# Inverse roots of batch 0's last two chunks on VectorE in Newton steps, with a new order of the whole kernel

## The chip, the core and the metric

One core of one Trainium2 chip runs the kernel. It has five engines that work side by side: TensorE (PE: matrix products, with weight loads, PEld, that overlap them), VectorE (DVE), ScalarE (ACT), GpSimd (POOL) and SyncE (SP, which here only issues transfers), and 16 DMA engines that move data. Every engine works through its own list of instructions in order; semaphores hold an instruction back until what it needs is there. The metric is the device time of one launch, in microseconds (us).

## The reference

For each of 8 batches and 8 heads, with 576 tokens of 64 numbers, a linear attention is computed and normalised by its root mean square; the heads are put side by side to 512 channels, and a gated linear unit with a causal convolution of 5 taps follows.

```python
kv  = einsum('bhsd,bhse->bhde', k, v)
out = einsum('bhsd,bhde->bhse', q, kv)
rms = sqrt(mean(out * out, axis=-1, keepdims=True) + 1e-06)
x   = out / rms * g_norm                     # then (B, S, H*D) = (8, 576, 512)

gate_pre = sum_k conv_w[k] * xp[:, k:k + S, :]   # xp: x with 4 zero rows ahead
gate = 1 / (1 + exp(-gate_pre))
val  = x @ w_val
return gate * val @ w_out
```

All numbers are float32, but the three weights come as float64, which the kernel narrows itself, in integer operations (`narrow_weight`).

## The kernel before

**Order.** The whole kernel is one list of named steps, `PLAN`, written out by a planner and run once, from first to last, under a manual schedule. A step issues its instructions on one engine (a DMA on a queue), and the place of a step in the list is its place on its engine. So the list fixes the order on every engine; nothing else moves.

**Chunks.** A batch's 576 tokens are cut into four whole chunks of 128 tokens, 0 to 3, and a last one, 4, of 64 tokens, whose eight heads are folded so that it fills 128 partitions with four heads each. In a step such as `sums 0 3` the first number is the batch and the second the chunk.

**One batch, step by step.**
- `load_half` (k and v), `load_q` or `load_q_rows`: loads, on SP's queue except a few on ScalarE's at the start. Only three blocks of q fit, and a load of q waits until the block that it overwrites has been turned.
- `kv_product b i` (PE, L435) makes k'v into the bank pair `raws`, and `kv_copy` (ACT, L443) copies it to SBUF.
- q is turned so that its head dimension lies on the partitions: for batches 0 and 1 by PE (`turn_q_rows`, L469, then `sort_q` on ACT, L476), for the others by VectorE (`turn_q`, L455).
- `raw_product` (L490) or `raw_pair` (L507), PE: q times kv, a chunk or a pair of them.
- `square` (ACT, L525) squares a chunk into one of two buffers, whose 65th column holds the epsilon; `sums` (DVE, L533) adds over each head, 8 numbers per token (4 for chunk 4); `powers` (POOL, L539) raises them to the power -0.5; `normalise` multiplies raw by the result: for batch 0 on VectorE (L555), for the others on ScalarE, a head at a time (L551).
- x is turned to channels on partitions: by PE (`turn_x`, L566, one PSUM buffer) and ScalarE (`keep_x`, L573) for batches 0 and 1 and for every chunk 4; otherwise by VectorE (`turn_blocks`, L579) and four DMAs on GpSimd's queue (`move_blocks`, L587).
- `halo` (POOL, L594) fills the rows ahead of the first token.
- The gate: `gate_start` (ACT, L598), four `gate_tap` (DVE, L604), `gate_end` (ACT, sigmoid, L611).
- The values: `val_product` and `keep_val` for batches 0 and 1 (PE L616, ACT L625); from batch 2 on seven products in place of eight by sums of operands (`val_fast`, L666; `x_sums`, `val_sums`, `val_keep`). `gated` (DVE, L629) multiplies by the gate.
- The output product: `out_product` (L697, L704), in the second half `fast_product` with sums (L763), then `keep_out` or `fast_keep`, and `store`.

**Around the change.** In batch 0 PE has little else to do while the first chunk goes from raw to x: the order on PE is the five raw products, `turn_x 0 3`, `turn_x 0 2`, `kv_product 1 0`, `turn_x 0 4`, two `turn_q_rows 1`, `turn_x 0 1`, and so on to the first `val_product 0 0 1`, whose weights `narrow_weight wval 0 0` to `0 7` must be done. `keep_warm` (L426) issues products that nobody uses; one stands ahead of `kv_product 0 1`, one behind it. The GpSimd list there is `powers 0 3`, `0 2`, `0 4`, `0 1`, `0 0`, `halo 0`. A number of `powers` results waits in one of three buffers.

Of the kernel before, what the change touches and what calls it, by code (L numbers as in the profile page):

```python
# [9 lines left out]
FP32 = mybir.dt.float32  # L10
# [5 lines left out]
P = 128  # L16
# [5 lines left out]
turn_q_rows 0 1; sort_q 0 0; narrow_weight cw 0 0; turn_q_rows 0 2; narrow_weight cw 0 1; narrow_weight cw 0 2;  # L22
turn_q_rows 0 3; narrow_weight cw 0 3; sort_q 0 1; narrow_weight cw 0 4; narrow_weight cw 0 5; turn_q_rows 0 4;
sort_q 0 2; narrow_weight cw 0 6; kv_product 0 0; narrow_weight cw 0 7; load_q_rows 1 0; sort_q 0 3;
load_half k 1 0; sort_q 0 4; load_half v 1 0; load_q_rows 1 1; keep_warm 1; kv_product 0 1; load_half k 1 1;
stage_weight wval 2; keep_warm 1; turn_cw; stage_weight wval 3; kv_copy 0; narrow_weight wval 1 0; load_half v 1 1; keep_cw;
narrow_weight wval 1 1; raw_product 0 3; load_half v 2 0; raw_product 0 2; square 0 3;
narrow_weight wval 1 2; raw_product 0 4; sums 0 3; load_half k 2 0; square 0 2; raw_product 0 1;
narrow_weight wval 0 0; powers 0 3; narrow_weight wval 1 3; sums 0 2; narrow_weight wval 0 1; raw_product 0 0;
load_half k 2 1; square 0 4; square 0 1; sums 0 4; powers 0 2; normalise 0 3; stage_weight wout 0; square 0 0;  # L30
narrow_weight wval 0 2; narrow_weight wval 1 4; turn_x 0 3; sums 0 1; narrow_weight wval 0 3; powers 0 4;
keep_x 0 3; normalise 0 2; narrow_weight wval 1 5; turn_x 0 2; powers 0 1; normalise 0 4; kv_product 1 0;
narrow_weight wval 1 6; keep_x 0 2; sums 0 0; turn_x 0 4; narrow_weight wval 0 4; turn_q_rows 1 0; powers 0 0;
keep_x 0 4; normalise 0 1; turn_q_rows 1 1; narrow_weight wval 0 5; sort_q 1 0; narrow_weight wval 1 7;
turn_x 0 1; halo 0; sort_q 1 1; normalise 0 0; turn_q_rows 1 2; keep_x 0 1; narrow_weight wval 2 0;
narrow_weight wval 0 6; narrow_weight wval 2 1; turn_x 0 0; narrow_weight wval 0 7; sort_q 1 2;
turn_q_rows 1 3; narrow_weight wval 3 0; narrow_weight wval 2 2; keep_x 0 0; turn_q_rows 1 4;
narrow_weight wval 2 3; kv_product 1 1; load_q 2 0; sort_q 1 3; narrow_weight wval 2 4; gate_start 0 0;
val_product 0 0 1; kv_copy 1; gate_tap 0 0 3; load_half v 2 1; sort_q 1 4; narrow_weight wval 3 1;
gate_tap 0 0 2; load_q 2 1; gate_start 0 1; raw_product 1 3; narrow_weight wval 2 5; gate_tap 0 0 1;  # L40
keep_val 0 0 1; raw_product 1 2; square 1 3; gate_tap 0 0 0; gate_start 0 2; val_product 0 1 1; sums 1 3;
square 1 2; narrow_weight wval 2 6; gate_end 0 0; powers 1 3; load_q 2 2; gate_tap 0 2 3;
narrow_weight wval 3 2; raw_product 1 1; sums 1 2; narrow_weight wval 3 3; gate_tap 0 1 3; raw_product 1 0;
keep_val 0 1 1; powers 1 2; stage_weight wout 2; square 1 1; normalise 1 3; val_product 0 0 0; sums 1 1;
narrow_weight wval 2 7; powers 1 1; gate_tap 0 2 2; square 1 0; turn_x 1 3; normalise 1 2; gate_tap 0 2 1;
val_product 0 1 0; sums 1 0; narrow_weight wout 0 0; keep_x 1 3; powers 1 0; narrow_weight wval 3 4;
narrow_weight wout 0 1; turn_x 1 2; narrow_weight wval 3 5; keep_val 0 0 0; raw_product 1 4; turn_q 2 0;
keep_x 1 2; kv_product 2 0; keep_val 0 1 0; narrow_weight wval 3 6; load_q 2 3; normalise 1 1; gate_tap 0 2 0;
kv_product 2 1; narrow_weight wval 3 7; square 1 4; stage_weight wout 3; val_sums 0; normalise 1 0; sums 1 4;
turn_x 1 1; turn_q 2 1; powers 1 4; val_product 0 2 1; keep_x 1 1; turn_q 2 2; load_q 3 0;  # L50
narrow_weight wout 0 2; gated 0 0; narrow_weight wout 0 3; turn_x 1 0; gate_tap 0 1 2; val_product 0 2 0;
keep_x 1 0; narrow_weight wout 2 0; gate_tap 0 1 1; load_half k 3 0; normalise 1 4; narrow_weight wout 0 4;
narrow_weight wout 2 1; turn_x 1 4; narrow_weight wout 0 5; val_product 0 3 1; gate_end 0 2; turn_q 2 3;
kv_copy 2; gate_tap 0 1 0; keep_x 1 4; keep_val 0 2 1; narrow_weight wout 0 6; raw_pair 2 3; keep_val 0 3 1;
narrow_weight wout 0 7; gate_start 0 3; stage_weight wout 1; load_half k 3 1; val_product 1 0 1; square 2 3;
load_q 3 1; narrow_weight wout 2 2; sums 2 3; square 2 2; narrow_weight wout 3 0; powers 2 3; gate_end 0 1;
gate_tap 0 3 3; val_product 0 3 0; narrow_weight wout 2 3; sums 2 2; keep_val 0 2 0; gated 0 1; load_q 3 2;
powers 2 2; narrow_weight wout 2 4; val_product 1 0 0; normalise 2 3; gate_tap 0 3 2; narrow_weight wout 2 5;
load_half v 3 0; gated 0 2; keep_val 0 3 0; halo 1; val_product 1 1 1; normalise 2 2; narrow_weight wout 2 6;
gate_tap 0 3 1; load_half v 3 1; narrow_weight wout 2 7; narrow_weight wout 3 1; raw_pair 2 1; turn_q 3 0;  # L60
keep_val 1 0 0; keep_val 1 0 1; narrow_weight wout 3 2; raw_product 2 4; narrow_weight wout 1 0;
turn_blocks 2 3; square 2 1; val_product 1 1 0; narrow_weight wout 1 1; load_q 3 3; sums 2 1; square 2 0;
turn_blocks 2 2; powers 2 1; narrow_weight wout 1 2; turn_q 3 1; val_product 1 2 1; square 2 4;
narrow_weight wout 3 3; sums 2 0; narrow_weight wout 1 3; narrow_weight wout 3 4; powers 2 0; gate_start 1 0;
gate_tap 0 3 0; val_product 1 2 0; normalise 2 1; narrow_weight wout 1 4; narrow_weight wout 1 5; sums 2 4;
normalise 2 0; val_product 1 3 1; narrow_weight wout 1 6; powers 2 4; narrow_weight wout 3 5; turn_blocks 2 1;
gate_end 0 3; narrow_weight wout 3 6; kv_product 3 0; keep_val 1 1 1; narrow_weight wout 1 7; normalise 2 4;
gate_tap 1 0 3; kv_product 3 1; gate_start 1 2; load_half k 4 0; gated 0 3; load_q 4 0; keep_val 1 1 0;
turn_blocks 2 0; turn_x 2 4; kv_copy 3; val_product 1 3 0; turn_q 3 2; gate_start 1 1; narrow_weight wout 3 7;
keep_val 1 2 1; gate_tap 1 0 2; keep_x 2 4; out_product 0 1; move_blocks 2 3; keep_val 1 3 0; gate_tap 1 1 3;  # L70
keep_val 1 2 0; turn_q 3 3; gate_tap 1 0 1; load_q 4 2; gate_tap 1 1 2; gate_tap 1 0 0; raw_pair 3 3;
load_half v 4 0; gate_tap 1 2 3; gate_end 1 0; out_product 0 0; gate_tap 1 1 1; square 3 2; keep_out 0 1;
gated 1 0; move_blocks 2 2; square 3 3; store 0 1; sums 3 2; gate_start 1 3; gate_tap 1 2 2; keep_val 1 3 1;
sums 3 3; out_product 0 2; gate_tap 1 1 0; keep_out 0 0; load_q 4 1; powers 3 3; gate_tap 1 3 3; gate_end 1 1;
gate_tap 1 2 1; load_half k 4 1; powers 3 2; gate_tap 1 2 0; normalise 3 3; gate_tap 1 3 2; out_product 0 3;
gated 1 1; store 0 0; gate_end 1 2; move_blocks 2 1; gate_tap 1 3 1; normalise 3 2; gate_tap 1 3 0; gated 1 2;
gate_end 1 3; raw_pair 3 1; gated 1 3; turn_q 4 0; raw_product 3 4; square 3 0; out_product 0 4; val_sums 1;
keep_out 0 3; load_q 4 3; square 3 1; sums 3 0; sums 3 1; square 3 4; powers 3 0; keep_out 0 2;
turn_blocks 3 3; store 0 3; weight_sums 0; weight_sums 1; out_product 0 7; powers 3 1; normalise 3 0;
val_sums 2; load_half v 4 1; weight_sums 2; turn_q 4 1; move_blocks 2 0; turn_blocks 3 2; turn_q 4 2;  # L80
store 0 2; normalise 3 1; out_product 0 5; sums 3 4; powers 3 4; keep_out 0 4; load_q 5 0; turn_blocks 3 1;
halo 2; turn_blocks 3 0; val_sums 3; kv_product 4 0; keep_out 0 5; turn_q 4 3; normalise 3 4; x_sums 2 0;
kv_product 4 1; load_half v 5 0; gate_start 2 2; x_sums 2 1; store 0 4; turn_x 3 4; gate_tap 2 2 3; kv_copy 4;
val_fast 2 0 0; keep_x 3 4; gate_tap 2 2 2; gate_start 2 1; val_fast 2 0 1; move_blocks 3 3; x_sums 2 2;
val_keep 2 0 0; load_q 5 1; keep_out 0 7; raw_pair 4 3; x_sums 2 3; gate_start 2 0; val_fast 2 0 2; square 4 3;
gate_tap 2 0 3; val_keep 2 0 1; store 0 5; sums 4 3; val_fast 2 0 3; val_keep 2 0 2; gate_tap 2 0 2;
square 4 2; powers 4 3; val_fast 2 0 4; sums 4 2; load_half k 5 0; val_fast 2 0 5; val_keep 2 0 4;
# [751 lines left out]
```

## Time and profile before

| | |
|---|---|
| median of 3 runs | 315.98 us (315.62 to 318.17) |
| the profiled execution | 316.86 us, its span 315.1 us |
| TensorE busy | 301.9 us (96% of the span), 3197 products |
| VectorE busy | 254.5 us (81%), 451 instructions |
| ScalarE busy | 191.6 us (61%), 542 |
| GpSimd busy | 138.0 us (44%), 177 |
| mean granted TensorE clock | 0.994 |
| powers, 128x8 (L539) | 32, mean 1910 ns |
| powers, 128x4 (L539) | 8, mean 1105 ns |
| sums, 128x8 (L533) | 32, mean 683 ns |
| normalise of a whole chunk on VectorE (L555) | 4, mean 684 ns |

How to read the profile: all times count from the start of the span. In a timeline a line gives start, duration, engine, line of the kernel, operation, output <- inputs, and how many instructions were merged into it (xN); in brackets stands how long the engine sat idle before it and what ended that. The page's slices cut the span into 40 equal parts of 7.9 us; a digit is the busy share in tenths. In tables of stretches the length comes first, then the busy time of each engine with its number of instructions, then the granted TensorE clock (1.00 is full), the busy share of the DMA engines and GB/s. Instructions of one VectorE or ScalarE list overlap a little, so they start closer together than their durations.

### The profile page before, as it was taken

What the parts mean: (1) busy time and instruction counts of PE and PEld (TensorE: products, weight loads), DVE (VectorE), ACT (ScalarE), POOL (GpSimd) and SP (SyncE); (2) the same over time, 40 slices, a digit from 0 to 9 for tenths busy, and PEclk for the clock granted to TensorE, in tenths of its full rate; (3) what the DMA queues carried; (4) which work ended last, traced back from release to release, by engine and by line L of the source; (5) the groups of instructions that cost most, each with busy time, mean ns of one, the idle gap of its engine ahead of it and who ended that gap; (6) DMA issues with size and microseconds to landing.
All of it is one profiled execution on the core that took longest, in us unless ns stands there. A gap on an engine that the chain in (4) does not pass through costs nothing.

```text
span 315.1 us, 8369 instructions
## 1 busy us (share of the span) xinstructions
PE 301.9 (96%) x3197; PEld 215.6 (68%) x3197; DVE 254.5 (81%) x451; ACT 191.6 (61%) x542; POOL 138.0 (44%) x177
## 2 busy tenths in 40 slices
PE   6878999999999999999999999999999999999994
PEld 6657877777645485757666766587668766888583
DVE  1159589999998889996989999899998689837512
ACT  2474899999586576856766678576752444233220
POOL 3047073266564835945594567477857000000000
PEclk9997999999999999999999999999999999999999
DMA  7999675794897779867987938402353212021333
GB/s 274 377 386 386 194 214 158 212 312 123 215 249 244 241 212 240 263 166 199 268 231 190 273 98 250 126 12 58 104 147 86 67 33 69 0 68 33 94 83 93
DMA packets 26696, 55.50 MB, mean 176 GB/s; under 512 B 6166, under 2 KB 8214, under 8 KB 26656
## 3 DMA queue, kind: packets, MB, share of 16 engines
q1 hardware_dynamic: 22608, 46.61, 50.9%
q0 software_dynamic: 3168, 6.32, 8.0%
q10 hardware_dynamic: 880, 2.03, 1.9%
q8 instruction: 25, 0.41, 0.6%
q14 instruction: 15, 0.12, 0.2%
HBM read 39.21 MB, written 9.44 MB: 154 GB/s over the span
## 4 chain that ended last, share of the span: by engine, by line
PE 88%; ACT 5%; DMA 4%; issue 1%; DVE 1%; ACTq 0%; DVEq 0%
PE out L697 18%; PE va L666 15%; PE val L616 8%; PE a L763 8%; PE vc L666 8%; PE cb L763 7%; PE raw L435 6%; PE out L704 5%; PE raw L507 4%; DMA v<-in_v_dram 4%; PE vb L666 4%; PE raw L490 3%; PE xTps L566 2%; ACT sq L525 1%; PE qTps L469 1%; ACT x L551 1%
## 5 line engine op out<-in xcount | busy, mean ns | idle before, releaser
L539 POOL TENSOR_TENSOR rt<-ss,mhalf 128x8 f32<-128x8 f32 (+1 forms) x40 | 69.7, 1749 | 86.8 <-DVE ss L533 83.8
L604 DVE SCALAR_TENSOR_TENSOR gate<-xT,cwT,gate 128x576 f32<-128x576 f32 x128 | 101.3, 810 | 4.3 <-ACT gate L598 3.5
L551 ACT ACTIVATE x<-raw,rt 128x64 f32<-128x64 f32 x252 | 55.7, 359 | 7.4 <-POOL rt L539 5.7
L587 POOL DMA_DIRECT2D xT<-y x96 | 52.9, 557 | 16.2 <-issue 5.3
L697 PE MATMUL out<-wout,gv 128*128 128x512 f32 x128 | 56.9, 594 | 0.0
L697 PEld LDWEIGHTS out<-wout,gv 128*128 128x128 f32 x128 | 24.1, 190 | 26.4 <-issue 24.8
L611 ACT ACTIVATE gate<-gate 128x576 f32<-128x576 f32 x32 | 22.1, 697 | 19.9 <-DVE gate L604 19.9
L533 DVE TENSOR_REDUCE ss<-sq 128x8 f32<-128x520 f32 (+1 forms) x40 | 24.9, 628 | 10.6 <-ACT sq L525 9.5
L616 PE MATMUL val<-xT,wval 128*128 128x288 f32 x128 | 33.0, 409 | 0.0
L525 ACT ACTIVATE sq<-raw 128x512 f32<-128x512 f32 (+1 forms) x40 | 22.1, 562 | 9.3 <-PE raw L507 6.0
L616 PEld LDWEIGHTS val<-xT,wval 128*128 128x128 f32 x128 | 23.6, 190 | 6.0 <-issue 0.2
L666 PE MATMUL va<-xs,vsum 128*128 128x288 f32 x96 | 27.3, 407 | 0.0
L598 ACT ACTIVATE gate<-xT,cwT 128x576 f32<-128x576 f32 x32 | 25.0, 789 | 0.3 <-DVE gv L629 0.2
L629 DVE TENSOR_TENSOR gv<-gv,gate 128x576 f32<-128x576 f32 x32 | 23.5, 750 | 0.5
L772 DVE TENSOR_TENSOR ot<-cb,ot 128x256 f32<-128x256 f32 x16 | 6.8, 422 | 19.0 <-PE cb L763 11.4
L666 PEld LDWEIGHTS va<-xs,vsum 128*128 128x128 f32 x96 | 18.2, 190 | 4.7
L435 PEld LDWEIGHTS raw<-v,k 64*64 64x64 f32 x1008 | 15.6, 135 | 6.9 <-issue 3.5
L712 ACT COPY ot<-out 128x512 f32<-128x512 f32 x20 | 11.8, 593 | 13.2 <-PE out L704 5.5
L435 PE MATMUL raw<-v,k 64*64 64x64 f32 x1008 | 16.8, 220 | 2.2 <-DMA v<-in_v_dram 1.4
L579 DVE STREAM_TRANSPOSE y<-x 128x512 f32<-128x512 f32 x24 | 16.5, 693 | 0.8 <-ACT x L551 0.8
L507 PEld LDWEIGHTS raw<-kvbd,qT 64*64 64x64 f32 x768 | 12.3, 134 | 7.0 <-issue 3.9
L455 DVE STREAM_TRANSPOSE qT<-qs 128x512 f32<-128x512 f32 x24 | 16.6, 690 | 0.0
(112 smaller groups left out, 501.0 us busy)
## 6 DMA issues: line engine op xcount, KB each, us to landing
qs<-in_q_dram SPq DMA_DIRECT2D x96, 140.0 KB, 4.8
out_dram<-ot SPq DMA_DIRECT2D x140, 64.0 KB, 1.8
k<-in_k_dram SPq DMA_DIRECT2D x14, 576.0 KB, 5.7
v<-in_v_dram SPq DMA_DIRECT2D x12, 576.0 KB, 6.4
xT<-y POOLq DMA_DIRECT2D x96, 64.0 KB, 3.8
y<-in_moe_w_val_dram SPq DMA_DIRECT2D x4, 512.0 KB, 12.5
w_wout<-in_moe_w_out_dram SPq DMA_DIRECT2D x4, 512.0 KB, 5.0
qs<-in_q_dram SPq DMA_DIRECT2D x3, 576.0 KB, 7.8
```

The costliest lines, as they stand in the source:

```text
L435: nc.tensor.matmul(raws[r * D:(r + 1) * D, s, i * D:(i + 1) * D], st["k", b, i][rows, r, cols], st["v", b, i][rows, r, cols], start=(j == ...
L507: nc.tensor.matmul(st["raw", b, x][cols, r, hp * D:(hp + 1) * D], st["qT", b][rows, hp, x * P + half * D:x * P + (half + 1) * D], kv_bd[b ...
L525: nc.scalar.activation(out=sq[:, 0:n, 0:D] if n < H or b < PAIRS else sq[:, :, 0:D].rearrange("p (r h) e -> p r h e", r=2), in_=by_head(b, ...
L539: nc.gpsimd.tensor_tensor(out=rt[:, 0:n], in0=st["ss", b, c][:, 0:n], in1=mhalf[:, 0:n], op=ALU.pow)
L551: nc.scalar.activation(out=x[:, to * D:(to + 1) * D], in_=one, func=AF.Copy, scale=st["rt", b, c][:, h:h + 1])
L587: nc.gpsimd.dma_start(out=xTs[b % 2][i * TB:(i + 1) * TB, :, first:first + P], in_=y[a * TB:(a + 1) * TB, i])
L598: nc.scalar.activation(out=gate[:], in_=xTs[b % 2][:, jt, HALO:SX], func=AF.Copy, scale=cwT[:, K - 1, jt:jt + 1])
L604: nc.vector.scalar_tensor_tensor(out=gate[:], in0=xTs[b % 2][:, jt, tap * TB:tap * TB + S], scalar=cwT[:, tap, jt:jt + 1], in1=gate[:], op ...
L616: nc.tensor.matmul(val[:], wval[:, kc, jt * P:(jt + 1) * P], xTs[b % 2][:, kc, HALO + n * SV:HALO + (n + 1) * SV], start=(kc == 0), stop=( ...
L666: nc.tensor.matmul(st[bank, "val", b, mj][:], weights_[:, k], tokens()[:, k], start=(n in (0, 1, 3) and k == 0), stop=(k == NK // 2 - 1), ...
L697: nc.tensor.matmul(po[:], gv[:, jt, first:first + P], wout[:, jt, :], start=(jt == 0), stop=(jt == NK - 1),)
L763: nc.tensor.matmul(st[bank, i, p], tokens()[:, k], weights_[:, k], start=(n < 2 and k == 0), stop=(k == NK // 2 - 1), skip_group_check=True)
```

## The change

Three things are edited. Chunks 1 and 0 of batch 0 get their inverse roots from a new step, `roots 0`, on VectorE, both together (16 numbers per partition): a first guess from the bit pattern, then three Newton steps. `sums` writes these two chunks' sums into the new tile `roots_of`, and `powers 0 1` and `powers 0 0` are gone from the list. The other three chunks of batch 0, and all other batches, keep `powers`.

```diff
+    NEWTON = (1, 0)
+    roots_of = const.tile([P, 3, len(NEWTON) * H], FP32, name="roots")
     def sums(b, c):
         n = heads(c)
-        ss = work.tile([P, H], FP32, tag="ss", bufs=3, name=f"ss{b}_{c}")
+        if b == 0 and c in NEWTON:
+            first = H * NEWTON.index(c)
+            ss, st["rt", b, c] = (roots_of[:, a, first:first + n] for a in (0, 1))
+        else:
+            ss = work.tile([P, H], FP32, tag="ss", bufs=3, name=f"ss{b}_{c}")
         nc.vector.reduce_sum(out=ss[:, 0:n], in_=st["sq", b, c][:, 0:n], axis=AX.X)
+    def roots(b):
+        s, y, a = (roots_of[:, n] for n in range(3))
+        nc.vector.tensor_scalar(
+            out=a.bitcast(U32), in0=s.bitcast(U32), scalar1=1, scalar2=None, op0=ALU.logical_shift_right)
+        nc.vector.tensor_scalar(
+            out=y.bitcast(U32), in0=a.bitcast(U32), scalar1=-1.0, scalar2=float(0x5F3759DF),
+            op0=ALU.mult, op1=ALU.add)
+        for _ in range(3):
+            nc.vector.scalar_tensor_tensor(out=a, in0=s, scalar=-0.5, in1=y, op0=ALU.mult, op1=ALU.mult)
+            nc.vector.tensor_tensor(out=a, in0=a, in1=y, op=ALU.mult)
+            nc.vector.scalar_tensor_tensor(out=y, in0=a, scalar=1.5, in1=y, op0=ALU.add, op1=ALU.mult)
```

The third edit is the list itself, planned anew from beginning to end: most steps stand at another place. The two lists have the same steps but for `roots 0`, the two `powers`, and `keep_warm 2` in place of two `keep_warm 1`. Here is the stretch around batch 0's roots on three engines, before (-) and after (+), other steps of the engine included:

```diff
 PE
-kv_product 0 0; keep_warm 1; kv_product 0 1; keep_warm 1; turn_cw; raw_product 0 3, 0 2, 0 4, 0 1, 0 0;
-turn_x 0 3; turn_x 0 2; kv_product 1 0; turn_x 0 4; turn_q_rows 1 0, 1 1; turn_x 0 1; turn_q_rows 1 2;
-turn_x 0 0; turn_q_rows 1 3, 1 4; kv_product 1 1; val_product 0 0 1
+kv_product 0 0; keep_warm 2; kv_product 0 1; turn_cw; raw_product 0 3, 0 2, 0 4, 0 1, 0 0;
+turn_x 0 3; turn_x 0 2; turn_q_rows 1 0; turn_x 0 4; turn_q_rows 1 1, 1 2; turn_x 0 1; kv_product 1 0;
+turn_x 0 0; turn_q_rows 1 3, 1 4; kv_product 1 1; val_product 0 0 1
 VectorE (wval: narrow_weight wval)
-wval 1 0; keep_cw; sums 0 3; wval 0 0; sums 0 2; sums 0 4; normalise 0 3; wval 1 4; sums 0 1; normalise 0 2;
-wval 1 5; normalise 0 4; wval 1 6; sums 0 0; wval 0 4; normalise 0 1; wval 0 5; wval 1 7; normalise 0 0
+keep_cw; wval 1 0; sums 0 3; sums 0 2; sums 0 4; wval 0 0; normalise 0 3; sums 0 1; sums 0 0; normalise 0 2;
+normalise 0 4; roots 0; normalise 0 1; normalise 0 0; wval 1 4; wval 0 4; wval 0 5; wval 1 5; wval 0 6;
+wval 0 7; wval 1 6; wval 1 7
 ScalarE
-kv_copy 0; wval 1 1; square 0 3; wval 1 2; square 0 2; wval 1 3; wval 0 1; square 0 4; square 0 1; square 0 0
+kv_copy 0; square 0 3; square 0 2; square 0 4; wval 1 1; square 0 1; wval 0 1; square 0 0
 SP (loads)
-load_half v 2 0, k 2 0, k 2 1; stage_weight wout 0; load_q 2 0; load_half v 2 1; load_q 2 1; load_q 2 2
+load_half v 2 0; stage_weight wout 0; load_half v 2 1; load_q 2 0; load_q 2 1; load_half k 2 0, k 2 1
```

Later in the list the changes are of the same kind: for example `val_sums 0` goes from about 51 us to behind batch 1's gates, `weight_sums 1` and `2` from about 102 us to between batch 2's and batch 3's values, the output products of batch 0 change places with each other, `kv_product` steps move past one or two others, and `move_blocks 2 0` goes ahead of batch 3's `powers 3 1`. The last fourteen products (`fast_product 3 2` and `3 3`) keep their order.

## The prediction

> **What bounds the kernel now.** I read the page's slices first, to see which engine is full where; then the stretches of two microseconds, for idle time and clock; then TensorE's timeline with the releasers of its gaps, and beside it the timelines of GpSimd and VectorE for what those gaps wait for.
>
> ```profile
> PE   6878999999999999999999999999999999999994
> DVE  1159589999998889996989999899998689837512
> POOL 3047073266564835945594567477857000000000
> PEclk9997999999999999999999999999999999999999
> ```
>
> TensorE (PE) is full from the fifth slice to the last but one. It is idle 13.2 us of the span (315.1 - 301.9), and only the third and fourth slices (16 to 32 us) lie near the change. The stretches there are: length, then the busy time of PE, weight loads, VectorE, ScalarE, GpSimd, then PE clock, DMA share and GB/s.
>
> ```profile
> 20.00:22.00 2.00, 1.33 (x12) 1.14 (x11) 1.15 (x3) 2.00 (x6) 1.79 (x2) 1.00 1.02 386
> 22.00:24.00 2.00, 0.66 (x4) 0.42 (x4) 1.99 (x4) 1.90 (x4) 2.00 (x2) 1.00 1.10 358
> 24.00:26.00 2.00, 0.97 (x4) 0.71 (x4) 2.00 (x5) 0.97 (x2) 2.00 (x2) 0.63 1.09 369
> 26.00:28.00 2.00, 2.00 (x73) 1.93 (x72) 2.00 (x5) 0.60 (x1) 1.33 (x2) 0.52 1.06 389
> ```
>
> PE idles 0.67 + 1.34 + 1.03 = 3.04 us here, and then runs at half clock. TensorE's timeline says what released it:
>
> ```profile
> 15.36 1.12 PE L426 MATMUL warm<-kvbd,ident 128*128 128x512 f32 x2
> 16.54 0.23 PE L405 MATMUL cwps<-ident,cw 21*128 21x21 f32 x1
> 16.71 4.63 PE L490 MATMUL raw<-kvbd,qT 128*128 128x128 f32 x40
> 23.09 0.66 PE L566 MATMUL xTps<-ident,x 128*128 128x128 f32 x4 [1.76 <-DVE x L555]
> 25.03 1.11 PE L566 MATMUL xTps<-ident,x 128*128 128x128 f32 x4 [1.28 <-ACT xT L573]
> 26.07 2.10 PE L435 MATMUL raw<-gv 64*64 64x64 f32 x72
> ...
> 35.24 2.21 PE L616 MATMUL val<-xT,wval 128*128 128x288 f32 x8
> ```
>
> The gaps wait for the first two normalised chunks, 3 and 2. Those wait for GpSimd's powers, four of them in one run and the last alone:
>
> ```profile
> 20.20 5.97 POOL L539 TENSOR_TENSOR rt<-ss,mhalf 128x8 f32<-128x8 f32 x4 [17.03 <-DVE ss L533]
> 26.85 1.95 POOL L539 TENSOR_TENSOR rt<-ss,mhalf 128x8 f32<-128x8 f32 x1 [0.67 <-DVE ss L533]
> ```
>
> Looked at one by one, the powers of chunks 3, 2, 4, 1 start at 20.20, 21.97, 23.58, 24.55 and take 1.78, 1.63, 1.00, 1.62. So the powers that the change takes away (chunks 1 and 0) are not the ones that PE waits for idle; those of 3, 2 and 4 stay. After 26 us PE has no gap up to 44.
>
> **The change, part by part.**
>
> *The new chain on VectorE.* Eleven instructions on 128x16, each but the first waiting for the one before. No row has that size. The nearest are the three small dependent scalings of the convolution weights, which start at 16.81, 17.01 and 17.28, thus 0.20 and 0.27 apart, and the 20x128 operations, up to 0.31 apart. At 0.22 each the chain is 2.4 us (bounds 2.2 to 3.4). The Trainium skill, page "VectorE: DVE Perf Modes", section "The TRN2 errata — SBUF-src ops pay a fixed extra latency per instruction", speaks against such a chain: every small instruction pays about 151 fixed cycles, so (16+151)/0.96 is an estimate of 0.17 us in place of 0.22, 1.9 us in place of 2.4. I keep the trace's spacing, since it includes the wait on the predecessor. Removed on GpSimd: 1.62 + 1.95 = 3.6 us.
>
> *The banks before the roots.* Both full-size warming products now lie before the second kv product, in a gap where PE waited 1.41 us for v. The cw transpose and the first raw product then start when the kv copy ends (16.23) and not behind a warming product (16.71): 0.45 us earlier, and all that follows with it. VectorE's sums come without a weight step between, and the squares too.
>
> *The path through batch 0.* With that 0.45: sums of chunk 3 at 18.97, powers 19.75 to 21.53, 23.16, 24.16 by the durations above. ScalarE's last square ends 22.3, so VectorE does normalise 3 (21.6 to 22.2), sums 1 and 0 (to 23.4), normalise 2 (to 24.05), normalise 4 (24.2 to 24.55), roots to 27.0, normalise 1 to 27.6, normalise 0 to 28.3. Before, the last two started at 27.22 and 28.83: 0.2 and 1.2 us earlier. PE: chunk 3's transposes at 22.3, chunk 2's at 24.1 (before 23.09 and 25.03), then a q turn 1.0, chunk 4 0.35, two q turns 2.0, so that chunk 1's transposes are reached at 28.0, when its x has been ready since 27.6. Then 0.6 + kv 1.2 + 0.6 + q turns 1.5 + kv 1.2: the first val product at 33.1 against 35.24, 2.1 us earlier. Its weights: eight steps of VectorE after 28.3, spaced 0.34 to 0.71; the sixth (wval 0 7) ends at 31.9, in time.
>
> *The clock.* Fine stretches show the clock full to 24.4, half from 24.6 to 27.8, full after 28.0: about 3.4 us, behind an equal stretch (21.1 to 24.5) in which PE was busy 0.9 us, 26%. Earlier stretches at some 58% (12 to 15.4) kept it. The skill, "TensorE: Matmul & The Clock Gate", Part 1, says that such windows are 3.4 us long and free-running, not tied to the kernel's start, and that an idle one halves the clock. In the new order the worst window holds 0.8 to 1.0 us of work, as low as before. Whether a window falls so is a matter of phase: with boundaries between about 20.0 and 21.6 it does, about half of the phases. Going by the trace's row alone, the half clock comes again and costs up to 1.6 us (PE is then full through it), and the val product starts at 34.7: 0.55 gained. By the rule it can be missed, and 2.1 are gained. I take the rule for the likeliest case, only just.
>
> *35 to 82 us.* PE's order is nearly the same. ScalarE now has four weight steps, two squares and two copies between the first square of batch 1 and its first normalise, which so ends at about 43.3 where PE wants it at 43.0: 0.3 us lost, where before 0.21 and 0.32 were. VectorE's list up to turn_q 2 3 is 1.3 us longer (the roots and one gate tap in; val_sums 0, gated 0 0 and one weight step out), but VectorE idled 2.70, 0.54, 0.58 and 0.52 us between 32 and 44, and starts earlier. Behind the sums of chunk 3 (19.6) stand 33.0 us of its work at the trace's spacings (0.60 for a 512-wide operation, 0.72 for a tap, 0.75 for a turn), and some 2.9 us of waits for powers, gates and squares: it ends turn_q 2 3 at about 55.5 against raw_pair 2 3 at 56.4 (58.6 - 2.1 - about 0.1). On SP, wout 0 and v 2 1 go ahead of q 2 0, and k 2 0 and k 2 1 go behind q 2 0 and q 2 1, that is behind eight DMAs (1.74 us of issue for four) that wait for batch 1's q turns. I put their issue at 36.7; the k loads of this stretch take 10.6 us to land, thus 47.3, against kv_product 2 0 at about 46.7: between 0 (the queue is emptier) and 1 us. I take 0.2. GpSimd's halo 0 now goes ahead of nothing that PE waits for.
>
> *82 us to the end.* PE is at 20.00 of 20.00 in almost every stretch, and what moves by a place or two (weight_sums, val_sums, keep_out, moves on POOL against powers) I cost at nothing: the cover is slack such as 1.7 us between gated 1 3 (ended 97.0) and the first product of batch 1 (98.6), and 2.2 us between normalise 3 1 (106.9) and kv 4 0 (109.1). The last 20 us have the same products, with the same three waits (292.2, 302.4, 308.8), since only one copy changes place.
>
> Sum: -2.1 + 0.2 - about 0.2 for the waits that shrink, -2.1. The profiled execution took 316.86 (span 315.1 and 1.76 around it), 0.9 above the median; the differences are taken from the median, so 315.98 - 2.1 = 313.9.
>
> **Rivals.**
> *Half clock again* (no gain): -0.55 in place of -2.1, and the mid-kernel waits vanish with the later arrival: 315.4. For it, the same idle pattern as before; against it, the phase.
> *VectorE becomes the bound* (slower). The place is VectorE's list from 24 to 97 us, which the slices show at 9 from 48 us on. Gated 1 3 has 2.2 to 2.4 us more work ahead of it (the roots; val_sums 0 moves but stays), and 1.7 us of slack. If no idle time is recovered, PE is late by 11c - 1.7, c being the time of one link: 0.7 us at c = 0.22, over 3.2 us from c = 0.44, and 4.0 us at c = 0.52: 320. For it: VectorE is full and each link waits. Against it: no small operation in the trace has links over 0.31, and the idle 4.3 us are there to be used.
> *The new order also removes other waits* (44.9, 47.7 and 137.9, together 0.21 + 0.32 + 0.77): 313.9 - 1.3 = 312.6, or 312.2 with the late k loads in time. The last of the three may be missing records only.
>
> **How the numbers follow.** The likeliest case, a lead of 2.1 us, 0.45 (its own range 312.4 to 315.0, with a part of it just over 1%); half clock again 0.22; more waits removed 0.13; VectorE as bound or a like new wait 0.20. 1% is 3.2 us, about what a measurement of this kernel can tell from no change. Faster than 312.8: 0.13 + 0.17 of the first case = 0.30. Slower than 319.1: 0.20. Within: 0.50. Range 311.5 to 319.7: below for all three early gains with a shorter chain, above up to VectorE at c = 0.5.
>
> **What would show it.** Right: the chain of roots at 2 to 3 us, the first val product at 33 to 33.5, no 3.4 us at half clock near 25 us, and raw_pair 2 3 at 56 to 57 (58.6 before). Wrong: links over 0.4 us, a PE gap before kv_product 2 0 released by DMA k, or gaps after 54 us released by VectorE.

## The result, and the profile after

| | before | after |
|---|---|---|
| median | 316.35 us (20 runs, beside those of after) | 314.97 us (20 runs) |
| range | 314.92 to 318.71 | 313.46 to 315.65 |
| ratio | | 0.9942, 95% interval 0.9921 to 0.9962 |
| profiled execution (its span) | 316.86 us (315.1) | 315.51 us (313.7) |
| TensorE busy | 301.9 us | 302.8 us |
| VectorE busy | 254.5 us, 451 instructions | 255.7 us, 462 |
| GpSimd busy | 138.0 us | 133.4 us |

The change makes the kernel 0.6% faster by the ratio, with an interval of 0.4 to 0.8%. The medians lie 1.4 us apart (0.4%), the means 1.8. The forecast was 313.9 and "within 1%". The times of after lie in two groups, eight at 313.5 to 314.0 and twelve at 314.9 to 315.7, with nothing between; the profiled execution is of the second group, and its first microseconds show one cause of that (below).

The page's slices of after, each 7.8 us:

```profile
PE   7978999999999999999999999999999999999993
DVE  1149899999999969899999899899998999764412
POOL 3033073435588456666684659265749000000000
PEclk9999999999999999999999999999999999999999
```

TensorE is full as before, and the dip in the clock row's fourth slice is gone. The stretches of two microseconds of after (columns as in the prediction):

```profile
22.00:24.00 2.00, 0.67 (x7) 0.48 (x5) 1.48 (x4) 1.75 (x4) 2.00 (x2) 1.00 1.10 358
24.00:26.00 2.00, 0.77 (x7) 0.45 (x5) 1.87 (x6) 1.66 (x3) 1.42 (x2) 1.00 1.09 366
26.00:28.00 2.00, 2.00 (x30) 1.60 (x30) 1.69 (x10) 2.00 (x5) 0.00 (x0) 1.00 1.08 403
```

TensorE is as idle here as before (0.67 and 0.77 us busy), but the granted clock stays at 1.00, where before it fell to 0.63 and 0.52. TensorE's timeline of after (start, duration, engine, line, operation, what was idle ahead of it and why):

```profile
1.36 4.05 PE L424 MATMUL warm<-ident 128*32 128x32 f32 x72 [1.36 <-POOL ident masks.py:199]
6.21 6.25 PE L472 MATMUL qTps<-ident,qs 128*64 128x128 f32 x72 [0.80 <-DMA qs<-in_q_dram]
...
15.52 1.28 PE L438 MATMUL raw<-v,k 64*64 64x64 f32 x72
16.73 0.23 PE L408 MATMUL cwps<-ident,cw 21*128 21x21 f32 x1
17.66 4.63 PE L493 MATMUL raw<-kvbd,qT 128*128 128x128 f32 x40 [0.70 <-ACT kvbd L446]
23.61 0.66 PE L587 MATMUL xTps<-ident,x 128*128 128x128 f32 x4 [1.33 <-DVE x L576]
25.51 0.63 PE L587 MATMUL xTps<-ident,x 128*128 128x128 f32 x4 [1.23 <-ACT wexp_wval L364]
```

The first raw product starts at 17.66 and not at the forecast 16.2, because batch 0's q turns took 6.25 us. Before, the same 72 products took 4.15:

```profile
6.32 4.15 PE L469 MATMUL qTps<-ident,qs 128*64 128x128 f32 x72 [1.41 <-DMA qs<-in_q_dram]
```

What the change does behind that is as forecast: GpSimd keeps three powers, and the Newton chain stands on VectorE. GpSimd's timeline of after:

```profile
21.16 4.26 POOL L546 TENSOR_TENSOR rt<-ss,mhalf 128x8 f32<-128x8 f32 x3 [18.00 <-DVE ss L540]
```

VectorE's timeline of after, the first and the last of the eleven links, and the two normalisations behind them:

```profile
25.79 0.17 DVE L554 TENSOR_SCALAR roots<-roots 128x16 uint32<-128x16 uint32 x1
25.99 0.17 DVE L556 TENSOR_SCALAR roots<-roots 128x16 uint32<-128x16 uint32 x1
26.20 0.18 DVE L560 SCALAR_TENSOR_TENSOR roots<-roots 128x16 f32<-128x16 f32 x1
...
27.88 0.17 DVE L562 SCALAR_TENSOR_TENSOR roots<-roots 128x16 f32<-128x16 f32 x1
28.15 1.29 DVE L576 TENSOR_TENSOR x<-raw,roots 128x512 f32<-128x512 f32 x2
```

A link lasts 0.17 us but starts 0.21 behind the one before; the chain is 25.79 to 28.05, 2.3 us.

**Where the 1.4 us come from.** Both timelines have the same products, so one can note by how much after is ahead at the same product:

| at the start of | before | after | ahead |
|---|---|---|---|
| first q turn | 6.32 | 6.21 | 0.11 |
| first raw product | 16.71 | 17.66 | -0.95 |
| first val product | 35.24 | 34.76 | 0.48 |
| `raw_pair 2 3` | 58.62 | 57.71 | 0.91 |
| `raw_pair 3 3` | 85.32 | 84.99 | 0.33 |
| `kv_product 5 0` | 135.55 | 135.22 | 0.33 |
| `raw_pair 5 3`, 0.97 us of a moved product taken out of after's | 142.69 | 141.33 | 1.36 |
| last product | 309.76 | 308.00 | 1.76 |
| end of the span | 315.1 | 313.7 | 1.4 |

The largest single step behind the first val product is at 138 us, far from the inverse roots. TensorE's timeline of before, then of after:

```profile
135.55 2.31 PE L435 MATMUL raw<-v,k 64*64 64x64 f32 x139
138.63 0.33 PE L435 MATMUL raw<-v,k 64*64 64x64 f32 x5 [0.77 <-issue]
```

```profile
135.22 2.33 PE L438 MATMUL raw<-v,k 64*64 64x64 f32 x144
137.48 3.70 PE L718 MATMUL out<-wout,gv 128*128 128x512 f32 x8
```

Before, TensorE stood still for 0.77 us five products before the end of batch 5's kv products, and waited for nothing that the profile shows ("issue"). After, the same 144 run through.

### The profile page after: what moved, and what is told of

The parts are those of the page before. It is cut to its first block, busy times and chain, and to the rows that moved or that the text cites. A ratio compares the mean times of both kernels' runs of the same rounds, so it can differ in the third digit from the quotient of the medians.

```text
span 313.7 us, 8362 instructions
## 1 busy us (share of the span) xinstructions
PE 302.8 (97%) x3197; PEld 217.6 (69%) x3197; DVE 255.7 (82%) x462; ACT 191.1 (61%) x542; POOL 133.4 (43%) x175
## 3 DMA queue, kind: packets, MB, share of 16 engines
q0 software_dynamic: 3168, 6.32, 7.9%
## 4 chain that ended last, share of the span: by engine, by line
PE 85%; ACT 5%; DMA 4%; DVE 2%; SPq 1%; issue 1%; POOL 1%; ACTq 0%; DVEq 0%
PE out L718 18%; PE va L687 15%; PE a L784 8%; PE vc L687 8%; PE cb L784 6%; PE val L637 6%; PE raw L438 5%; PE out L725 5%; PE raw L510 4%; PE vb L687 4%; PE qTps L472 3%; PE raw L493 2%; DMA k<-in_k_dram 2%; DMA qs<-in_q_dram 2%; PE xTps L587 1%; ACT x L572 1%
## 5 line engine op out<-in xcount | busy, mean ns | idle before, releaser
L546 POOL TENSOR_TENSOR rt<-ss,mhalf 128x8 f32<-128x8 f32 (+1 forms) x38 | 65.4, 1728 | 80.7 <-DVE ss L540 77.1
L540 DVE TENSOR_REDUCE ss<-sq 128x8 f32<-128x520 f32 (+1 forms) x38 | 23.3, 626 | 8.3 <-ACT sq L528 8.1
L650 DVE TENSOR_TENSOR gv<-gv,gate 128x576 f32<-128x576 f32 x32 | 24.2, 762 | 3.0 <-ACT gate L632 2.8
L615 POOL COPY xT<-xT 128x124 f32<-128x124 f32 x32 | 13.4, 456 | 10.3 <-ACT xT L594 10.3
L708 ACT COPY gv<-va 128x288 f32<-128x288 f32 x12 | 4.8, 400 | 19.8 <-PE va L687 19.8
```

Of the source, the lines that this page charges most:

```text
L540: nc.vector.reduce_sum(out=ss[:, 0:n], in_=st["sq", b, c][:, 0:n], axis=AX.X)
L546: nc.gpsimd.tensor_tensor(out=rt[:, 0:n], in0=st["ss", b, c][:, 0:n], in1=mhalf[:, 0:n], op=ALU.pow)
L650: nc.vector.tensor_tensor(out=both, in0=both, in1=st["gate", b, jt][:], op=ALU.mult)
```

## The experiments

Every ratio is against the kernel before, on the same chip and in the same rounds. The first four share 35 runs of it (median 316.27), the next four 26 (316.50), the next three 29 (316.39), the last 17 (316.28).

**Taking the change apart.** The new list without the Newton chain:

```diff
-    NEWTON = (1, 0)
+    NEWTON = ()
-powers 0 4; normalise 0 2;
+powers 0 4; powers 0 1; powers 0 0; normalise 0 2;
...
-turn_q_rows 1 0; roots 0; keep_x 0 2;
+turn_q_rows 1 0; keep_x 0 2;
```

> The new order as it is, but chunks 1 and 0 of batch 0 get their roots on GpSimd again (two powers behind the third, in place of the Newton steps). Theory (the roots were hidden behind TensorE's own work, the gain is the order's): ratio to before 0.994 to 0.996, the first val product within 0.3 us of the changed kernel's 34.8 us, since chunk 1's powers end near 27.1 and its transposes start at 29.4. Rival (the Newton steps carry the gain): 0.999 to 1.001, with a TensorE gap ahead of chunk 1's or chunk 0's transposes.

315.53 us, 0.9967 (0.9947 to 0.9987): over half of the gain is there without the chain, though the ratio is a little above the expected 0.994 to 0.996. The first val product starts at 35.00, and no gap lies ahead of chunk 1's or chunk 0's transposes, as the theory had it. Its profile caught the half clock again (stretches of this run):

```profile
22.00:24.00 2.00, 0.66 (x4) 0.42 (x4) 1.68 (x4) 1.45 (x3) 2.00 (x2) 1.00 1.09 355
24.00:26.00 2.00, 1.41 (x12) 1.24 (x14) 1.05 (x3) 1.61 (x4) 2.00 (x3) 0.76 1.08 371
26.00:28.00 2.00, 2.00 (x18) 1.34 (x16) 0.55 (x2) 1.27 (x3) 1.29 (x1) 0.50 1.07 395
```

The stretch from 22 to 24 is as idle as after's, to 0.01 us; the one run keeps its clock and the other doesn't. And VectorE's timeline of this run shows a wait that nobody had named:

```profile
22.14 0.68 DVE L530 TENSOR_REDUCE ss<-sq 128x8 f32<-128x520 f32 x1
23.15 0.69 DVE L530 TENSOR_REDUCE ss<-sq 128x8 f32<-128x520 f32 x1 [0.32 <-POOL rt L536]
23.76 1.01 DVE L566 TENSOR_TENSOR x<-raw,rt 128x512 f32<-128x512 f32 x2
```

`sums 0 0`, the fifth sum, waits for GpSimd, since only three buffers hold sums and it needs that of chunk 2; behind it `normalise 0 2` is late, and TensorE's transposes of chunk 2 start at 24.59, 2.31 us behind chunk 3's (1.90 in after). The roots take two of the five sums out of this ring. The last experiment tests that.

The old list with the Newton chain in place of two powers:

```diff
-turn_x 0 2; powers 0 1; normalise 0 4;
+turn_x 0 2; normalise 0 4;
...
-sums 0 0; turn_x 0 4; narrow_weight wval 0 4; turn_q_rows 1 0; powers 0 0;
+sums 0 0; roots 0; turn_x 0 4; narrow_weight wval 0 4; turn_q_rows 1 0;
```

> The old order as it is, but with the Newton steps for chunks 1 and 0 right behind the last sums and without their two powers. Theory: nothing gained and nothing lost, ratio 0.999 to 1.001; the chain takes 2.3 us of VectorE, makes chunk 1's x some 1.5 us later (29 us), still ahead of its transposes at 30.4. Rival (the Newton steps carry the gain): 0.994 to 0.996.

316.79 us, 1.0025 (1.0010 to 1.0040): without the new order the chain gains nothing. Its first val product starts at 35.40 (35.24 before); TensorE waits for chunk 3 as before, 1.76 us. Eight of its twelve runs had a mean granted clock under 0.997, against 18 of the 35 runs of before. So the small loss need not be the chain's own.

The new list up to the first val product with the old behind it, and the reverse:

```diff
 PLAN
-(steps of the new list behind val_product 0 0 1)
+(the remaining steps, in the order of the old list)
```

> The new list up to the first val product (with the Newton steps and both warming products together), then all steps not yet issued in the old order. Theory (about half of the gain comes from the stage up to 35 us, half from waits that the later order removes): ratio 0.996 to 0.998. Rival (all of it comes from the head): 0.994. Rival (all from the later order): 1.000.

> The old list up to the first val product (powers on GpSimd for all five chunks), then all steps not yet issued in the new order. Theory (half and half): 0.996 to 0.998, with the gap of 0.77 us near 138 us gone. Rival (all from the head): 1.000. Rival (all from the later order): 0.994.

315.32 us, 0.9986 (0.9965 to 1.0007), and 315.78 us, 0.9984 (0.9961 to 1.0007): neither half has a gain that can be told from none, and the two do not add up to 0.9942 clearly. Both intervals leave out 0.994, so neither half alone carries the whole gain; between the expected 0.996 to 0.998 and no gain they do not decide. Each has a seam: at it the first raw product of batch 1 waits for ScalarE's kv copy, 0.33 and 0.44 us. The new head with the old tail shows the stall at 138 (0.55 us), the old head with the new tail doesn't. So that part of the gain belongs to the tail, and it has nothing to do with the roots.

**What the stall is.** The stall has the same place in three profiles with the old tail. Two runs have 14 more small warming products at the start, which also tests what is wrong with after's first microseconds:

```diff
-start_warm 36
+start_warm 50
```

> The changed kernel with 50 instead of 36 small warming products at the start (14 more, in the gap before q arrives). Theory (the spread of the changed kernel's runs, and the 6.25 us that its first q turns took in the profile against 4.15 before, is TensorE starting at a half rate that the clock row does not show, because a part of the start was idle): the first q turns take about 4.2 us, and the median falls by 0.5 to 1.5 us, to 313.5 to 314.5. Rival (the slow start comes from q arriving late, or has a phase that warming does not touch): the median stays at 315.0 and q turns over 5 us are still seen.

315.79 us, 0.999 (0.997 to 1.001): the expected 313.5 to 314.5 did not come. Its first q turns do take 4.15 us. But TensorE's timeline shows what ate that:

```profile
6.58 4.15 PE L462 MATMUL qTps<-ident,qs 128*64 128x128 f32 x72
...
12.36 0.57 PE L428 MATMUL raw<-v,k 64*64 64x64 f32 x21 [0.67 <-issue]
...
31.38 0.56 PE L428 MATMUL raw<-gv 64*64 64x64 f32 x20 [1.15 <-issue]
```

Two new stalls "for nothing", 1.8 us together, again inside rows of small products. Counting the product records from the start (the xN of the timeline's lines), they lie behind records 223 and 475.

> The kernel before with the same 14 more warming products. Theory of the start: half of the fills in phase, 0 to 1 us faster than before. Theory of the stall (the 0.77 us in which TensorE waits for nothing shown at 137.9 us is a wait for instructions, and so lies at a fixed number of instructions from the start): with some 56 more TensorE instructions ahead, the stall moves to earlier products, or to a place where it is hidden; 0 to 0.8 us gained. Rival (it is a wait for data of kv_product 5, or missing records): the stall stays behind the same product, the 139th of 144, at about 137.9 us.

316.89 us, 1.0012 (0.9992 to 1.0032). The stall at 138 is gone, but time is lost at two earlier places (TensorE's timeline of this run):

```profile
10.01 1.62 PE L427 MATMUL raw<-v,k 64*64 64x64 f32 x72
...
30.97 0.60 PE L558 MATMUL xTps<-ident,x 128*128 128x128 f32 x4 [0.83 <-ACT qT L468]
```

Record 223 lies in the first row, which takes 1.62 us in place of 1.28 (a wait for v behind it covers that), and the second wait lies exactly behind record 475: the two counts of the run above. The profile puts the second down to ScalarE's copy of q. In before the same transposes start without a gap, right behind their own copy, so the wait for instructions is the likelier cause. What is fetched by then? The page's list of DMA queues for the kernel before has a queue of its own for instructions:

```profile
q8 instruction: 25, 0.41, 0.6%
```

25 transfers of 0.41 MB / 25 = 16 KB. TensorE has 3197 products and as many weight loads, 6394 instructions, and 6394 / 25 = 256. So this queue brings TensorE's instructions, one block for every 256 of them. The places of the stalls agree: from record 223 to 475 are 504 instructions, from 475 to that of the stall at 138, 1872, are 2794, which makes 2 blocks of 252 and 11 of 254. The Trainium skill, "Runtime: NRT & Kernel Launch", section "Instruction fetch mechanics", has the same block (16 KiB, 256 instructions) and calls the cost of crossing a boundary "mostly hidden". For most of the 25 no stall is seen here either; but a row of 64x64 products runs through 72 records, 144 instructions, in 1.28 us, a whole block in 2.3 us. In the narrow stretches of the DMA view the transfer lies at 135.9 in before, 2.7 us ahead of the stall's end (138.63); at 29.0 in the run above, 2.4 us ahead of 31.38; at 130.3 in this run, in the slow val products ahead of the kv products, and there nothing waits.

A direct test: four records more at the start must move the stall by four products, wherever k and v are.

```diff
-start_warm 36
+start_warm 38
```

> The kernel before with 38 instead of 36 small warming products, four product records more ahead of everything. Theory (the stall at 137.9 us is TensorE's wait for its next block of instructions, whose end lies at product record 1873 from the start): the stall keeps that count and so falls behind the 135th of kv_product 5's 144 records and not the 139th, with 0.4 to 0.8 us, and a transfer on the instruction queue some 2.5 us ahead of its end. Rival (it waits for k or v of batch 5, or records are missing): it stays behind the 139th. Median within 0.3 us of before either way.

316.45 us, 1.0003 (0.9985 to 1.0022). TensorE's timeline:

```profile
135.67 2.21 PE L427 MATMUL raw<-v,k 64*64 64x64 f32 x135
138.45 0.35 PE L427 MATMUL raw<-v,k 64*64 64x64 f32 x9 [0.57 <-issue]
```

Behind the 135th, as expected: behind record 1872 from the start, as in before. The transfer lay at 136.1, 2.4 us ahead of the end. The stall is a wait for instructions, and its place is set by the number of instructions ahead of it. Whether TensorE waits there depends on when the transfer comes. In after, record 1872 is again the 139th of kv_product 5's 144, so a shift of the count is not what freed it: its transfer lay at 134.6, 2.7 us ahead of the next product, while in before it lay at 135.9, 1.9 us ahead of where that product would have been. Why it came earlier in the new order, no run shows.

**Pieces of the new order.** TensorE switches between kv products (64x64) and whole ones twice more in after, because `val_product 1 3 0` and `turn_x 2 4` stand between batch 3's two kv products. Joined:

```diff
-kv_product 3 0;
+kv_product 3 0; kv_product 3 1;
...
 val_product 1 3 0;
...
-turn_x 2 4; kv_product 3 1;
+turn_x 2 4;
```

> The changed kernel with kv_product 3 1 moved directly behind kv_product 3 0, ahead of val_product 1 3 0 and turn_x 2 4, as adjacent as it was before. Theory (the lead over the kernel before shrinks by 0.58 us between 58 and 85 us because TensorE switches twice more between 64x64 and 128x128 products there, about 0.2 us each): raw_pair 3 3 comes 0.4 to 0.5 us earlier (84.6), median 0.3 to 0.5 us lower than the changed kernel's 315.0. Rival (the 0.58 us is lost elsewhere, or k 3 1 is not loaded in time): no gain, or a wait ahead of kv_product 3 1.

314.01 us (6 runs), 0.9929 (0.9906 to 0.9952). From `raw_pair 2 3` to `raw_pair 3 3` it takes 83.00 - 56.08 = 26.92 us, after 84.99 - 57.71 = 27.28, before 85.32 - 58.62 = 26.70. So 0.36 of the 0.58 us that after loses there is the split kv product. TensorE's timeline, which matters for the prediction too: its list up to 70 us is after's, but its start is not slow.

```profile
6.08 4.33 PE L462 MATMUL qTps<-ident,qs 128*64 128x128 f32 x72 [0.82 <-DMA qs<-in_q_dram]
...
15.90 4.63 PE L483 MATMUL raw<-kvbd,qT 128*128 128x128 f32 x40 [0.68 <-ACT kvbd L436]
21.85 0.65 PE L577 MATMUL xTps<-ident,x 128*128 128x128 f32 x4 [1.33 <-DVE x L566]
...
30.68 1.31 PE L462 MATMUL qTps<-ident,qs 128*64 128x128 f32 x20 [0.27 <-issue]
...
33.13 2.21 PE L627 MATMUL val<-xT,wval 128*128 128x288 f32 x8
```

The first val product starts at 33.13. (The 0.27 us are a wait for instructions again, at record 475.)

The second warming product back behind `kv_product 0 1`:

```diff
-keep_warm 2; kv_product 0 1; stage_weight wval 3; turn_cw;
+keep_warm 1; kv_product 0 1; stage_weight wval 3; keep_warm 1; turn_cw;
```

> The changed kernel with the second full-size warming product back behind kv_product 0 1, where it was before. By the prediction's sum raw_product 0 3 then starts 0.45 us later behind the warming product, and the first val product 0.45 later; median +0.4, at 315.4. Rival (the wait for ScalarE's kv copy, 0.70 us in the changed kernel's profile, sets that start): 0.1 us or less.

314.51 us, 0.996 (0.9938 to 0.9983). The first raw product starts at 16.32, against 15.90 in the run above, and the first val product at 33.54 against 33.13: 0.42 and 0.41 us, where the sum had 0.45. The medians do not separate that.

The joined kernel, with the instruction blocks shifted:

```diff
-start_warm 36
+start_warm 30
-kv_product 3 0;
+kv_product 3 0; kv_product 3 1;
...
 val_product 1 3 0;
...
-turn_x 2 4; kv_product 3 1;
+turn_x 2 4;
```

> The changed kernel with kv_product 3 joined as in the run before, and 30 instead of 36 small warming products. Theory of the blocks: record 475, at which 0.25 to 0.27 us were lost among batch 1's q turns, now lies 12 records later among them, and the stall there is gone; 0.2 to 0.3 us gained over the joined kernel (fastest runs 313.3), if no later block falls badly. Rival (fewer warming products leave TensorE at its slow start more often): more runs with first q turns over 5 us and a median above 314.0.

314.51 us, 0.9945 (0.9926 to 0.9964), its fastest run 312.98. The stall at record 475 is gone (all 24 q turns in 1.53 us), but the profiled start was the slow one, 5.91 us for the first q turns. No gain over the joined kernel can be shown. Nor is the shift proved as the cause: the runs with six Newton steps and with powers and five buffers (below) have the old count, and their 24 q turns take 1.53 us too.

**What the Newton chain costs and brings.** Three more Newton steps:

```diff
-        for _ in range(3):
+        for _ in range(6):
```

> The changed kernel with six Newton steps in place of three: nine more small operations on VectorE, 9 x 0.21 = 1.9 us, results equal. Theory (the chain has 0.55 us of cover ahead of chunk 1's transposes and 1.75 ahead of chunk 0's in the changed kernel's profile, and VectorE ends turn_q 2 3 just ahead of raw_pair 2 3): chunk 1's transposes wait some 1.3 us, and the median rises by 1.3 to 1.9 us, to about 316.5. The prediction's rival (VectorE has 1.7 us of slack and idle time to recover): under 0.7 us.

315.12 us, 0.9975 (0.9953 to 0.9997). TensorE's timeline:

```profile
30.77 0.63 PE L577 MATMUL xTps<-ident,x 128*128 128x128 f32 x4 [1.56 <-DVE x L566]
```

Chunk 1's transposes wait 1.56 us. Its first q turns end 0.21 us earlier than after's; with that taken out, these transposes are 30.77 - 29.15 = 1.62 us late, and the first val product is 35.79 - 34.55 = 1.24 us late, and so are `raw_pair 2 3` (58.74 - 57.50) and, at 1.21, the last product (309.00 - 307.79). The x they need comes 2.0 us later, so 0.38 us of the longer chain was covered. The other 0.38 came back behind chunk 0's transposes, where after loses about as much at record 475 (1.89 us for 24 q turns) and this run doesn't (1.53). The list of VectorE behind it absorbs the longer chain without one new wait of TensorE. The ratio is 0.33% worse than after's, 1.0 us; the expected median of 316.5 was too high.

The joined kernel with powers in place of roots, and five buffers for sums:

```diff
-    NEWTON = (1, 0)
+    NEWTON = ()
-            ss = work.tile([P, H], FP32, tag="ss", bufs=3, name=f"ss{b}_{c}")
+            ss = work.tile([P, H], FP32, tag="ss", bufs=5, name=f"ss{b}_{c}")
-powers 0 4; normalise 0 2;
+powers 0 4; powers 0 1; powers 0 0; normalise 0 2;
...
-turn_q_rows 1 0; roots 0; keep_x 0 2;
+turn_q_rows 1 0; keep_x 0 2;
```

> The joined kernel (new order, kv_product 3 in one piece) with GpSimd's two powers in place of the Newton steps, and five buffers for the sums in place of three. In the run of the new order with powers, sums 0 0 had waited 0.32 us for a buffer that GpSimd still read, and chunk 2's transposes came 2.31 us behind chunk 3's and not 1.89. Theory (the roots brought no time by being faster, only by taking two chunks out of the ring of three buffers): with five buffers the step from chunk 3's transposes to chunk 2's is 1.9 us, no gap lies ahead of chunk 1's or chunk 0's, and the ratio is that of the joined kernel with roots, 0.993 within 0.2%. Rival (GpSimd's powers are too slow for chunks 1 and 0 in the new order): a gap of over 0.3 us ahead of their transposes, released by VectorE's normalise, and a ratio of 0.996 or more.

314.83 us, 0.9948 (0.992 to 0.9977). TensorE's timeline:

```profile
6.21 6.38 PE L462 MATMUL qTps<-ident,qs 128*64 128x128 f32 x72 [0.79 <-DMA qs<-in_q_dram]
...
23.74 0.66 PE L577 MATMUL xTps<-ident,x 128*128 128x128 f32 x4 [1.33 <-DVE x L566]
25.63 0.63 PE L577 MATMUL xTps<-ident,x 128*128 128x128 f32 x4 [1.23 <-ACT wexp_wval L354]
...
31.27 0.66 PE L577 MATMUL xTps<-ident,x 128*128 128x128 f32 x4
```

Chunk 2's transposes follow chunk 3's by 1.89 us, and chunk 0's by 7.53; in the joined kernel with roots it is 1.89 and 7.54 (21.85 to 29.39), in after 1.90 and 7.54. No gap lies between. So on TensorE's path GpSimd's two powers are as good as the Newton chain, once the sums have buffers enough. The ratio is within the expected 0.2% of the joined kernel's, and its interval takes in both theories' values: the trace decides here. By the times alone a small gain of the roots isn't excluded: both versions with powers lie about 0.2% above theirs with roots (0.9967 against 0.9942, 0.9948 against 0.9929), with intervals that overlap.

## Why the prediction was right

The median, 314.97, is 1.1 us above the forecast 313.9. Within 1% was the likeliest case, and the mechanism at the start was the one described; but the size came together from terms that nearly cancel, which is luck.

- *Which powers TensorE waits for.* Right: it still waits 1.33 and 1.23 us for chunks 3 and 2, whose powers stayed.
- *The chain, 0.22 a link, 2.4 us.* Measured 0.21 and 2.3. The 0.17 us worked out from the Trainium skill, "VectorE: DVE Perf Modes", section "The TRN2 errata — SBUF-src ops pay a fixed extra latency per instruction", is the length of one link, 0.17 to 0.18 here; what counts for a chain is the spacing.
- *The warming products, 0.45.* Measured 0.42, but with a quick start only. In after's slow one the gap that they were to fill is not there: `kv_product 0 1` follows them at 15.52 without a wait. With one warming product less ahead of it (0.95 us), and before's 2.56 us from there to the first raw product, that product would have started at about 17.1 and not at 17.66. That is an estimate from these timelines; no run has the old place together with a slow start.
- *The path to the first val product, 33.1, 2.1 us earlier.* Right where the start is as before's: 33.13 in the joined kernel, whose list is the same up to there. In after's own profile it is 34.76, 0.48 earlier only. The step that failed is an unwritten one: that TensorE's first microseconds stay as they were in before. The products of the first q turns give it away (after's stretches of these instructions; length, busy TensorE, weight loads, ScalarE, then the clock):

```profile
9.50:10.00 0.50, 0.50 (x8) 0.50 (x6) 0.21 (x2) 1.00 1.17 415
...
10.50:11.00 0.50, 0.50 (x14) 0.50 (x12) 0.03 (x1) 1.00 1.03 387
```

  Eight to ten products in half a microsecond up to 10.5, then fourteen, as in before's q turns throughout, while the clock row says 1.00 for both. The Trainium skill, "TensorE: Matmul & The Clock Gate", Part 1, has TensorE cold at half speed until a free-running window of some 3.4 us was busy. That fits: after's warming products never got faster and end at 5.4, 0.8 us ahead of q. Before's went from 14 to 20 per half microsecond at 4.0. The list does not decide it, since up to the q turns TensorE's steps are the same in both, and with the new head the same 72 products took 4.15 to 4.33 us in three other profiles (powers, joined, warming product moved back) and 5.9 to 6.4 in four; with the old head they took 4.15 in three and 4.95 in one. That it is the phase is the reading that fits best; no run tests it. The slow start explains only a part of the second group of after's times: four of its twelve runs have a granted clock of 0.991 to 0.995, the half clock, and eight have the full one. For these eight the joined kernel's profile, 1.63 us ahead of after's at the first val product, makes the slow start likely; it wasn't shown.
- *The clock near 25 us.* Taken as missed, only just, and it was missed in after's profile. In a mean granted clock under 0.997 it shows in 4 of after's 20 runs and in 18 of 35 runs of before; between these two kinds of before's runs lie 0.86 us (316.61 and 315.75), where the prediction had up to 1.6. After's four have a median of 314.97, 1.3 us above its faster group. The run of the new list with powers, with the same idle stretch and half clock, supports the rule of the phase, as against the trace's row alone.
- *35 to 82 us.* The wait at `turn_x 1 3` was 0.19 in place of 0.3, and that ahead of `turn_x 1 2` (0.32) vanished, as the third rival had it; the k loads of batch 2 were in time (0 and not 0.2). What was not seen is the split of batch 3's kv products, "PE's order is nearly the same": 0.58 us lost between 58 and 85, of which 0.36 go when it is joined.
- *82 us to the end, "at nothing".* Here the term was mis-sized most: 1.4 us were gained (from 0.33 to 1.76 us ahead at the last product). 0.77 of them are the stall at 138, which the prediction took for possibly missing records. Whether it comes hangs on the time of an instruction transfer, which no step of the list names. The other 0.66, from `kv_product 5 0` to the end, were neither tested nor traced to a cause.
- *Sum.* 2.1 at the start, less 1.6 for the slow start, plus 0.4 up to `raw_pair 2 3`, less 0.6 behind it, plus 1.4 later, less 0.4 at the last stores: 1.3, or 1.4 unrounded.
- *Rivals.* Half clock again: not in after's profile, but in that of the new list with powers. VectorE as the bound: excluded, since even six Newton steps cost TensorE only their uncovered part at the first transposes and nothing later. Other waits removed: two of the three it named went, at 47.7 and 137.9; the one at 44.9 stayed (0.19).
- *Slips in the sums.* With the late k loads in time 312.6 becomes 312.4 and not 312.2; at c = 0.44 the formula gives 3.1 and not over 3.2; the slack behind gated 1 3 is 1.6 and not 1.7. None of them moves the forecast.

No version was shown to beat after. The joined kernel is 0.36 us faster in the trace, with an interval that overlaps after's.

## What to carry to other kernels

Before you replace a slow operation, see whether anybody waits for it, and what else it holds: here a ring of three buffers, not the power's 1.7 us, was what the new order would have run into. Compare two traces by how far one is ahead at the same product; a gain far from the edit asks for a cause of its own. Where a dense row of small products stalls for "issue", count the instructions ahead of it: a shift by eight instructions moved it here with the count, and a shift by 56 took it from one place and brought losses at two others. Shifting is no cure by itself, since whether the engine waits also hangs on when the block's transfer comes.

## What the runs showed of the hardware

- TensorE's instructions come in blocks of 256 (25 transfers of 16 KB for 6394 instructions). In rows of 64x64 products and q turns, at 9 and 29 ns an instruction, the next block can be late by 0.25 to 1.15 us. The wait ended 2.4 to 2.7 us behind the block's transfer (135.9 to 138.63, 29.0 to 31.38, 136.1 to 138.45); where the transfer came 2.7 us ahead of the product, in after at 134.6, there was none.
- Small dependent VectorE operations on 128x16 take 0.17 to 0.18 us each and start 0.20 to 0.21 us apart, in all eleven links of after.
- At the start, TensorE can run its products at 8 to 10 per half microsecond in place of 14 for four microseconds, with a granted clock of 1.00 in the row.
- Behind a stretch of two microseconds with 0.66 to 0.67 us of work the clock fell to about half in two profiles (before and the new list with powers) and stayed full in after's.
